# One PSUM bank instead of two for the output products of layer A's segments, and half of the first tail spread moved behind the last rows and their store

## The chip, the core and the metric

The kernel runs on one core of one Trainium2 chip. The metric is the device time of one execution in microseconds (us); the median of the runs counts. A profiled execution gives a trace of its own, with its own time and its span (from its first to its last instruction).

## The reference: what is computed

The input x (2048 rows of 640 values, bf16) goes through four residual layers, A, B, A, B:

```python
x = x + A(layernorm(x)); x = x + B(layernorm(x))
x = x + A(layernorm(x)); x = x + B(layernorm(x))
```

Layer A is attention with a recurrent memory. The rows are cut into 64 segments of 32. For each segment the 8 memory rows and the 32 segment rows are stacked (h, 40 rows), projected to q, k and v with 32 heads of 192 values, masked, put through a softmax, and multiplied by Wo (6144 x 640). The first 8 output rows are the memory of the next segment, the other 32 are the layer's output:

```python
for s in range(n_seg):
    h = jnp.concatenate([mem, xs], axis=1)
    q, k, v = (einsum('btd,dhe->bhte', h, W) for W in (Wq, Wk, Wv))
    p = softmax(where(mask, einsum('bhqe,bhke->bhqk', q, k) * scale, -1e9))
    o = einsum('bhte,hed->btd', einsum('bhqk,bhke->bhqe', p, v), Wo)
    mem = o[:, :M]
    outs.append(o[:, M:])
```

Layer B is linear attention with softmax feature maps over 32 heads of 20 values; it is a chain of large products that needs all rows of layer A's output. The function returns the rows after the fourth layer.

## The kernel before

**The stages.** `run` calls `layer_A` and `layer_B` in turn. `layer_A` consists of `A_pre`, which projects the last 8 rows of every segment in large products, and `A_chain`, which walks through the 64 segments one after the other, because each needs the memory that the one before it leaves. In `A_chain` the order of the instructions on every engine is the order in which they are written (`manual_schedule`); in layer B a scheduler orders them at compile time.

**A segment of the chain.** The 32 heads are worked off in four rounds. A round projects q, k and v (L1092), turns them, forms scores (L1129), exponentials (L1218) and the weighted values (L1142), scales these rows (L1172) and multiplies them by the round's part of Wo into the PSUM tile `ps_w` (L1198, `wo_round`). All four rounds of a segment add into one `ps_w`. The first product into it is issued in round n = 1 of the loop, and the last after the loop. Then the kernel turns `ps_w` (L1371) and adds halves of it (L1373), which gives the memory rows in `hT`. At the start of the next segment `keep_rows(W_done)` reads the same `ps_w` again: two copies on ScalarE into `wh` (L1051) and two additions on VectorE into `orow` (L1054, `under`); `store_rows` sends `orow` to DRAM from the GpSimd queue (L1058). So the tile of one segment is still read when the next has begun, and `ps_w` had two buffers (`bufs=2`).

**The tails.** The output rows 24 to 31 of each segment aren't multiplied in the chain. Their scaled, turned rows (`tail_rows` L1183, `turn_tail` L1187, `store_tail` L1191) go to a DRAM tensor `otb`, and layer B does their products for 16 segments at a time in four blocks tb = 0 to 3 before its own work: `fetch_tails` loads a block (L1388, 1536 KB on the sync queue), `spread_tails` copies it into the layout that TensorE wants (eight copies of 128 x 768 values: two for each round r = 0 to 3, L97 on VectorE for the letter "v", L99 on ScalarE for "s"), and `multiply` runs 48 steps c, each one product of 512 columns into a bank `kv0` or `kv1` (L1421) and one of 128 columns into `ps_post` (L1422). Step c uses the spread of round c // 12. The results leave through `obB` (L1424, L1425, stored by L1427). Later steps of layer B's first part are the block loads of x (L384) and of layer A's output (L389, added on GpSimd by L390), and, in the first layer B only, a fusion of weights (L186, L427, weights loaded by L523) between the steps of blocks 1 and 2.

**The junction.** In the last segment of the chain, block 0 is already fetched during the rounds and its spread is issued with the letters "vvss" straight after the last rows are turned and before the last `wo_round`: rounds 0 and 1 on VectorE, 2 and 3 on ScalarE. After it come the last `wo_round`, four products that only keep TensorE busy (L1205), and after the loop the last tail, `keep_rows` and `store_rows`. The spread of block 1 is issued in layer B behind them. There are two junctions from a layer A to a layer B.

**The banks.** PSUM has eight banks, and the built program shows which tile lies where. In the chain before the change: `ps_qk_q` 0, `ps_qk_k` 1, `ps_w` 2 (even segments) and 3 (odd segments), `ps_v` and `ps_o1` 4, `ps_s` and `ps_idle` 5, `ps_o` 6, `ps_t` 7. In layer B: `kv0` 0, `kv1` 1, `kv2` 2, `ps_post` (and later tiles of the same pool) 3, the other tiles 4 to 7. The last segment has number 63. A tile that lies where an earlier one did waits for the last reader of that one.

Of the kernel before, what the change touches and what calls it, by code (L numbers as in the profile page):

```python
# [8 lines left out]
P = 128  # L9
BF16 = mybir.dt.bfloat16  # L10
F32 = mybir.dt.float32
# [26 lines left out]
def ap3(ap, dims):  # L38
    return bass.AP(tensor=ap.tensor, offset=ap.offset, ap=[list(d) for d in dims])
# [86 lines left out]
class Kernel:  # L126
# [876 lines left out]
    def A_chain(self, xn_dram, at_dram, li, load_slot, piece, late_wo, load_both, wo, low):  # L1003
# [3 lines left out]
        with tc.tile_pool(name=f"A{li}_ch", reuse_waits="tile", bufs=1) as sp, \  # L1007
# [17 lines left out]
            u, w, ut, wt = self.factors()  # L1025
# [10 lines left out]
            def rounds(s):  # L1036
                return range(NR) if s % 2 == 0 else range(NR - 1, -1, -1)
# [9 lines left out]

            def keep_rows(W):
                half = sp.tile([P, 160], F32, name="wh", tag="E")
                for a in range(2):  # L1050
                    nc.scalar.activation(out=half[64 * a:64 * a + 64, :], in_=W[64:P, 160 * a:160 * a + 160], func=ACT.Copy)  # L1051
                for a in range(2):
                    h = slice(64 * a, 64 * a + 64)
                    last = nc.vector.tensor_tensor(out=orow[h, :], in0=W[0:64, 160 * a:160 * a + 160], in1=half[h, :], op=ALU.add)  # L1054
                self.chain_end.append(last)

            def store_rows(s):
                nc.gpsimd.dma_start(out=self.rows_d[32 * s:32 * s + 32, :].rearrange("t (q f) -> q t f", q=4), in_=orow)  # L1058
# [133 lines left out]

            def wo_round(W, r, OT, first, last, part=range(12)):
                for i in part:
                    for g in range(2):
                        q = 32 * (2 * (i % 2) + g)
                        rhs = wo[r, i].rearrange("p (a g f) -> p a g f", a=2, g=2)[:, :, g, :]
                        step = nc.tensor.matmul(W[q:q + 32, 0:320], lhsT=OT[i // 6][:, i % 6 // 2, 32 * (i % 2):32 * (i % 2) + 32],  # L1198
                                         rhs=rhs, start=(first and i < OWN + 2), stop=(last and i in part[-2:]), tile_position=(0, q),
                                         skip_group_check=True)  # L1200
                return step
# [38 lines left out]
            kqs.append(load_kqb(0, rounds(0)[3]))  # L1240
            load_rows(1)
            for s in range(NSEG):
                W = pop.tile([P, 512], F32, name="ps_w", tag="w", bufs=2)
                order = rounds(s)
                L = NR - 1

# [50 lines left out]
                def output_steps(n):  # L1297
                    for j, i in outs[0:n]:
                        wo_round(W, order[j], OTs[j], False, False, range(i, i + 2))
                    del outs[0:n]  # L1300

                for n in range(L):
# [6 lines left out]
                    if n == 1:  # L1309
                        step = wo_round(W, order[0], OTs[0], True, False, range(OWN, 12))  # L1310
                        if s == NSEG - 1:
# [3 lines left out]
                            tails = self.kept_tails  # L1315
# [41 lines left out]
                turn(L, oscs)  # L1357
                output_steps(len(outs))
                if s == NSEG - 1:
                    self.first_tails = tails, [self.spread_tails(0, tails[0], low, "vvss")]  # L1360
                if s + 1 < NSEG:
                    if s + 2 < NSEG:
                        load_rows(s + 2)
# [13 lines left out]
            store_tail(turn_tail(tail_rows(rct, "OTh"), ots[1][:, 0:192]), NSEG - 1, order[L])  # L1377
            keep_rows(W_done)
            store_rows(NSEG - 1)

    def keep_tails(self, tb, low):
        self.kept_tails.append(self.fetch_tails(tb, low))
        return self.tails_load
# [7 lines left out]
    def spread_tails(self, tb, ot, low, engines="vsvs"):  # L1391
        o = 7680 + 12288 * (tb % 2)
        ow = low[:, o + 6144:o + 12288].rearrange("p (r j s x) -> p r j s x", r=4, j=6, x=16)
        for r in range(4):
            for b in range(2):
                at = 192 * (r // 2) + (0 if (r + b) % 2 else 16)
                o = ow[:, r, :, b:16:2, :]
                i = ot[:, b:16:2, at:at + 16]
                i = ap3(i, [list(i.ap[0]), [32, 6], *[list(d) for d in i.ap[1:]]])
                self.ev.copy(out=o, in_=i, eng=engines[r])  # L1400
        return ow
# [64 lines left out]
```

## Time and profile before

| what | value |
|---|---|
| median of 3 runs | 3265.13 us (3263.06, 3265.13, 3274.89) |
| the profiled execution | 3262.61 us, span 3260.9 us |
| mean granted TensorE clock | 0.993 |
| TensorE products busy | 3093.0 us, 95% of the span |
| VectorE, ScalarE, GpSimd busy | 68%, 58%, 43% of the span |
| bytes moved by DMA | 747.58 MB, 229 GB/s on the mean |

In the rows of the profile PE is TensorE's products, PEld its weight loads, DVE VectorE, ACT ScalarE, POOL GpSimd and SPq the sync engine's queue. A row of the timeline has the start in us from the beginning of the span, the duration, the engine, the line, the operation, what is written and read, the shapes and the number of instructions that were merged; in square brackets stands how long the engine sat idle before it and what released it. The four layers take about the stretches 0 to 1374 (A), 1374 to 1643 (B), 1643 to 3003 (A) and 3003 to the end (B).

### The profile page before, as it was taken

The page shows a single profiled execution, that of the slowest core. Times are in us where ns is not written, and L with a number is a line of the kernel's source. Part 1 is how long each engine was busy: PE and PEld are TensorE (multiplying, and loading weights), DVE is VectorE, ACT ScalarE, POOL GpSimd, SP SyncE. Part 2 cuts the span into 40 slices and gives each one's busy share as a digit, 9 for nine tenths or more (in the row PEclk, how much of TensorE's full clock was granted, in tenths as well). Part 3 has the DMA queues.
Part 4 walks back from the last instruction along what each step waited for, and adds up shares of the span by engine and source line. Part 5 has one row for each costly group of instructions (what it writes and reads, how often), then busy time and mean ns, then how long its engine had stood idle before and what let it go on. Part 6 is the DMA issues. An engine that isn't in the chain of part 4 may idle for free.

```text
span 3260.9 us, 140891 instructions
## 1 busy us (share of the span) xinstructions
PE 3093.0 (95%) x59424; PEld 1976.8 (61%) x59730; DVE 2207.3 (68%) x5457; ACT 1882.7 (58%) x4481; POOL 1411.0 (43%) x2920
## 2 busy tenths in 40 slices
PE   9989999999999999899999899999999999998999
PEld 7756666666666666555367566666666666665553
DVE  5557777777777777656643577777777777776565
ACT  3346666666666666546433466666666666666453
POOL 3345555555555554430122355555555555554300
PEclk9999999999999999999999999999999999999999
DMA  8977777777777777840385777777777777778300
GB/s 301 379 274 261 239 252 250 237 256 248 244 260 235 258 248 244 278 155 1 112 318 192 241 239 264 245 256 242 254 253 244 260 238 253 249 245 284 129 1 33
DMA packets 325018, 747.58 MB, mean 229 GB/s; under 512 B 65818, under 2 KB 100274, under 8 KB 321314
## 3 DMA queue, kind: packets, MB, share of 16 engines
q1 hardware_dynamic: 254850, 638.55, 56.3%
q0 software_dynamic: 67616, 86.77, 9.6%
q10 hardware_dynamic: 1920, 13.24, 1.0%
q8 instruction: 469, 7.68, 1.0%
q14 instruction: 163, 1.34, 0.1%
HBM read 668.80 MB, written 77.03 MB: 229 GB/s over the span
## 4 chain that ended last, share of the span: by engine, by line
PE 75%; DMA 11%; DVE 7%; ACT 3%; issue 3%; POOL 0%; SPq 0%; PEld 0%; DVEq 0%; POOLq 0%; ACTq 0%
PE ps_qk_q L1092 12%; PE ps_qk_k L1092 12%; PE ps_v L1092 11%; PE ps_w L1198 10%; PE ps_pre L960 6%; PE ps_s L1129 5%; DMA arena<-in_A_Wv_dram 5%; DMA Vp<-vb 3%; PE ps_pre L989 3%; PE ps_o L1142 3%; PE kv L1421 2%; DMA arena<-wo_rows 2%; DVE raws L1371 2%; PE ps_wo L444 2%; DVE hT L1373 2%
## 5 line engine op out<-in xcount | busy, mean ns | idle before, releaser
L1092 PEld LDWEIGHTS <-hT 128*32 128x32 bf16 x30720 | 790.0, 97 | 422.7 <-issue 40.3
L1112 DVE STREAM_TRANSPOSE QK<-raws 128x512 bf16<-128x512 bf16 (+1 forms) x1152 | 730.4, 642 | 205.5 <-ACT raws L1107 171.4
L1092 PE MATMUL ps_qk_q<-arena,hT 128*32 128x384 bf16 x10240 | 508.5, 327 | 36.3 <-DVE hT L1373 30.4
L1092 PE MATMUL ps_qk_k<-arena,hT 128*32 128x384 bf16 x10240 | 510.0, 328 | 5.4 <-DMA arena<-in_A_Wk_dram 2.3
L1069 POOL COPY QK<-kqb 64x192 bf16<-64x192 bf16 x1024 | 350.4, 342 | 376.7 <-PE ps_s L1129 340.1
L1107 ACT ACTIVATE raws<-ps_qk_k 128x512 bf16<-128x512 f32 (+1 forms) x640 | 313.5, 510 | 253.5 <-PE ps_qk_k L1092 253.5
L1092 PE MATMUL ps_v<-arena,hT 128*32 128x384 bf16 x8192 | 436.0, 327 | 14.3 <-issue 6.8
L1073 POOL DMA_DIRECT2D Vp<-vb x512 | 257.6, 503 | 417.0 <-PE ps_t L1155 252.3
L1172 ACT ACTIVATE raws<-ps_o,rc 128x192 bf16<-128x192 f32 x1024 | 373.7, 420 | 109.8 <-DVE rc L1166 107.5
L1107 ACT ACTIVATE raws<-ps_qk_q 128x512 bf16<-128x512 f32 x512 | 305.7, 597 | 162.5 <-PE ps_qk_q L1092 151.2
L1062 POOL DMA_DIRECT2D kqb<-kqb x512 | 290.6, 568 | 70.9 <-POOL QK L1069 50.2
L1198 PE MATMUL ps_w<-arena,under 128*32 128x320 bf16 x6144 | 306.2, 300 | 11.9 <-issue 8.8
L1121 DVE CAST Vp<-ps_v 64x384 bf16<-64x384 f32 x512 | 286.3, 559 | 38.3 <-ACT Vp L1119 23.0
L1129 PEld LDWEIGHTS <-QK 128*80 128x80 bf16 x4096 | 195.5, 120 | 160.8 <-issue 156.6
L1119 ACT ACTIVATE Vp<-ps_v 64x384 bf16<-64x384 f32 x512 | 246.4, 481 | 55.6 <-PE ps_v L1092 54.8
L1129 PE MATMUL ps_s<-QK 128*80 128x80 bf16 x4096 | 256.4, 210 | 3.8 <-POOL QK L1069 2.8
L1218 ACT ACTIVATE E<-ps_s 80x320 bf16<-80x320 f32 x512 | 217.6, 425 | 30.7 <-PE ps_t L1155 27.7
L1051 ACT ACTIVATE wh<-ps_w 64x160 f32<-64x160 f32 x256 | 76.6, 299 | 266.1 <-DVE raws L1371 256.2
L1058 POOL DMA_DIRECT2D attn<-under x128 | 91.6, 716 | 294.2 <-DVE under L1054 291.3
L960 PEld LDWEIGHTS <-arena 128*128 128x128 bf16 x1920 | 188.4, 98 | 31.6 <-DVE next_xT L97 4.6
L97 DVE CAST arena<-ps_pre 128x512 bf16<-128x512 f32 (+1 forms) x160 | 102.2, 646 | 143.2 <-PE ps_pre L960 96.2
L1142 PE MATMUL ps_o<-Vp,E 80*32 80x193 bf16 x4096 | 179.9, 248 | 18.1 <-DMA Vp<-vb 7.4
(159 smaller groups left out, 4580.7 us busy)
## 6 DMA issues: line engine op xcount, KB each, us to landing
arena<-wo_rows SPq DMA_DIRECT2D x560, 320.0 KB, 5.5
arena<-in_A_Wq_dram SPq DMA_DIRECT2D x427, 384.0 KB, 4.2
arena<-in_A_Wk_dram SPq DMA_DIRECT2D x298, 384.0 KB, 4.7
arena<-in_A_Wv_dram SPq DMA_DIRECT2D x290, 384.0 KB, 6.0
kqb<-kqb POOLq DMA_DIRECT2D x512, 48.0 KB, 4.9
vb<-arena POOLq DMA_DIRECT2D x128, 97.0 KB, 6.1
Vp<-vb POOLq DMA_DIRECT2D x512, 24.2 KB, 4.0
kqb<-arena SPq DMA_DIRECT2D x8, 1536.0 KB, 9.7
```

The costliest lines, as they stand in the source:

```text
L960: nc.tensor.matmul(ps[:, T * i:T * i + T], lhsT=w[b][:, P * c:P * c + P], rhs=xBT[:, b, :], start=(b == 0), stop=(b == KC - 1))
L1062: nc.gpsimd.dma_start(out=kqb[:], in_=self.kqb_d[r, :, s, :])
L1069: nc.gpsimd.tensor_copy(out=o, in_=kqb[h, :].rearrange("p (x c q) -> p x c q", c=3, q=16))
L1073: nc.gpsimd.dma_start(out=Vs[n % 2][64:80, :], in_=self.vb_d[s, r].rearrange("g t f -> (g t) f"))
L1092: last = nc.tensor.matmul(o, lhsT=hT[:, b, :], rhs=rhs, start=(i == 0), stop=(i == KC - 1), tile_position=(0, 32 * g), skip_group_check=True)
L1107: nc.scalar.activation(out=raw[:, c], in_=ps[:, c], func=ACT.Copy)
L1112: nc.vector.transpose(out=o, in_=i)
L1121: nc.vector.tensor_copy(out=o, in_=i)
L1129: nc.tensor.matmul(S[0:80, c0:c0 + 80], lhsT=KT[:, 4 * x + c, :], rhs=QT[:, 4 * x + c, :], start=(c % 2 == 0), stop=(c % 2 == 1), skip_gro ...
L1142: nc.tensor.matmul(O[G][32 * h:32 * h + 32, VH * G:VH * G + 193], lhsT=E[0:80, 80 * h + 32 * G:80 * h + 32 * G + 32], rhs=V[0:80, VH * h:V ...
L1172: nc.scalar.activation(out=out, in_=i, func=ACT.Copy, scale=rc[G])
L1198: step = nc.tensor.matmul(W[q:q + 32, 0:320], lhsT=OT[i // 6][:, i % 6 // 2, 32 * (i % 2):32 * (i % 2) + 32], rhs=rhs, start=(first and i ...
```

## The change

The tile `ps_w` gets the one buffer that its pool has by default, and the spread of block 0 is issued in two halves: rounds 0 and 1 on VectorE where all four stood before, rounds 2 and 3 on ScalarE after the last rows are kept and stored. `spread_tails` leaves out the rounds whose letter is a blank.

```diff
             for s in range(NSEG):
-                W = pop.tile([P, 512], F32, name="ps_w", tag="w", bufs=2)
+                W = pop.tile([P, 512], F32, name="ps_w", tag="w")
...
                 if s == NSEG - 1:
-                    self.first_tails = tails, [self.spread_tails(0, tails[0], low, "vvss")]
+                    self.spread_tails(0, tails[0], low, "vv")
...
             store_tail(turn_tail(tail_rows(rct, "OTh"), ots[1][:, 0:192]), NSEG - 1, order[L])
             keep_rows(W_done)
             store_rows(NSEG - 1)
+            self.first_tails = tails, [self.spread_tails(0, tails[0], low, "  ss")]
...
         for r in range(4):
+            if engines[r:r + 1] in ("", " "):
+                continue
             for b in range(2):
```

In the built program the chain's banks become: `ps_qk_q` 0, `ps_qk_k` 1, `ps_w` 2, `ps_v` and `ps_o1` 3, `ps_s` and `ps_idle` 4, `ps_o` 5, `ps_t` 6; bank 7 is free in the chain. Layer B's banks stay as they were. The order of TensorE's instructions is the same as before. On ScalarE `otr` (L1183) and the two `wh` copies (L1051) of the last segment now stand ahead of the four spread copies. In layer B the scheduler moves a few instructions: VectorE's copies for the spread of block 2 stand behind two more weight copies, a weight store on GpSimd one addition earlier, and in the second layer B the store of block 1's rows (L1427) ahead of one load of layer A's rows (L389) on the sync queue.

## Prediction

> **What bounds the kernel now.** I start at the page: TensorE's products cover 95% of the span, so a change can only pay where TensorE stands still or runs at a lower clock. The change touches two places: the bank of `ps_w` in all 128 segments, and the two junctions from a chain to a layer B. For the chain I ask the instructions of L1054, the last reader of `ps_w`, who waited for them:
>
> ```profile
> span 3260.9 us, 140891 instructions
> PE 3093.0 (95%) x59424; PEld 1976.8 (61%) x59730; DVE 2207.3 (68%) x5457; ACT 1882.7 (58%) x4481; POOL 1411.0 (43%) x2920
> ...
> who waited for it (us, times):
>   POOL attn L1058: 291.3, 126
>   PE ps_post L1422: 15.7, 2
> ```
>
> In 126 segments only the store waited for it, never TensorE. TensorE waited twice, for 15.7 us in all: at the two junctions, with `ps_post`. The timeline of the first junction shows why.
>
> ```profile
> 1372.98 1.03 PE L1205 MATMUL ps_idle<-arena,ident 128*32 128x512 bf16 x4
> ...
> 1376.81 3.04 ACT L99 ACTIVATE arena<-arena 128x768 bf16<-128x768 bf16 x4 [4.81 <-DMA arena<-otb]
> 1376.83 1.16 DVE L97 COPY arena<-arena 128x768 bf16<-128x768 bf16 x4 [4.41 <-DMA arena<-otb]
> 1377.51 0.10 PEld L1421 LDWEIGHTS <-arena 128*128 128x128 bf16 x1 [3.49 <-DVE arena L97]
> 1377.91 0.16 DVE L1178 RECIPROCAL rct<-ps_t 128x1 f32<-128x1 f32 x1
> 1379.76 0.40 ACT L1183 ACTIVATE otr<-ps_t,rct 128x192 bf16<-128x192 f32 x1
> 1380.19 0.61 ACT L1051 ACTIVATE wh<-ps_w 64x160 f32<-64x160 f32 x2
> ...
> 1380.83 0.65 DVE L1054 TENSOR_TENSOR under<-ps_w,wh 64x160 bf16<-64x160 f32 x2 [0.26 <-ACT wh L1051]
> ...
> 1381.62 0.27 PE L1422 MATMUL ps_post<-arena 128*128 128x128 bf16 x1 [7.61 <-DVE under L1054]
> ...
> 1381.68 0.63 PE L1421 MATMUL kv<-arena 128*128 128x512 bf16 x1
> ...
> 1382.11 0.31 PE L1422 MATMUL ps_post<-arena 128*128 128x128 bf16 x1
> ```
>
> TensorE is done with the chain at 1374.01. The tail block lands at 1376.8; VectorE spreads round 0, and TensorE's first weights for block 0 go at 1377.51. The first `kv0` product can follow; `ps_post` can't. It lies in bank 3, the last segment's `ps_w` too, so it waits until `keep_rows` has read that. `keep_rows` is late because its ScalarE copies stand behind four spread copies (3.04 us) and the tail row. The idle time thus has two halves: up to 1377.5 it is the load, from there to 1381.62 the bank. The second junction is the same:
>
> ```profile
> 3002.05 1.03 PE L1205 MATMUL ps_idle<-arena,ident 128*32 128x512 bf16 x4
> ...
> 3007.10 0.10 PEld L1421 LDWEIGHTS <-arena 128*128 128x128 bf16 x1 [4.01 <-DVE arena L97]
> 3007.50 0.16 DVE L1178 RECIPROCAL rct<-ps_t 128x1 f32<-128x1 f32 x1
> ...
> 3011.20 0.26 PE L1422 MATMUL ps_post<-arena 128*128 128x128 bf16 x1 [8.12 <-DVE under L1054]
> ```
>
> Three more stretches of the timeline are needed for the parts: the last reader of `ps_o1` at the junction, a segment in the middle of the chain, and the pace of TensorE in block 0 at full clock.
>
> ```profile
> 1371.59 0.41 ACT L1172 ACTIVATE raws<-ps_o,rc 128x192 bf16<-128x192 f32 x1
> ```
>
> ```profile
> 1000.64 0.65 DVE L1054 TENSOR_TENSOR under<-ps_w,wh 64x160 bf16<-64x160 f32 x2
> ...
> 1007.45 0.73 PE L1198 MATMUL ps_w<-arena,under 128*32 128x320 bf16 x16
> ```
>
> ```profile
> 1384.80 0.38 PE L1421 MATMUL kv<-arena 128*128 128x512 bf16 x1
> ...
> 1385.07 0.38 PE L1421 MATMUL kv<-arena 128*128 128x512 bf16 x1
> ```
>
> **Part 1, one bank.** At the junction `ps_post` now lies where the chain had `ps_v` and `ps_o1`. The last reader of that bank on ScalarE is L1172 of the last round, which ends at 1372.0, before TensorE is idle at all. So the first `ps_post` follows its `kv0` product. The weight load at 1377.51 takes 0.10, and from a `kv0` product to its `ps_post` pass 0.43 us at half clock (1381.68 to 1382.11) and about half of that, 0.21, at full clock. Junction one, where the clock is still full: 1377.51 + 0.10 + 0.21 = 1377.82 against 1381.62, **3.80 us earlier**. Junction two, at half clock by then: 3007.10 + 0.10 + 0.43 = 3007.63 against 3011.20, **3.57 us earlier**. Sum 7.4.
>
> In the chain the single bank adds a dependence: the first product of a segment must follow the last read of the segment before. In the segment at 1000 us the read ends at 1001.29 and the first product starts at 1007.45, so 6.16 us are to spare. TensorE issues in order, and that product waits already for its round's transposes on VectorE, behind L1054 in the same queue, so the built program gets no further wait there. I cost it at nothing. Without that cover each 0.1 us would cost 12.6 us over 126 segments.
>
> **Part 2, the spread in halves.** VectorE is unchanged: rounds 0 and 1 end at 1377.99, `rct` at 1378.07. ScalarE is then free, so the tail row runs from 1378.1 to 1378.5, `wh` to 1379.13, L1054 to about 1379.8, and the two stores leave 1.65 us earlier. Nobody on TensorE waits for these now. The four copies follow on ScalarE from 1379.13, two by 1380.7 and all by 1382.2, instead of 1379.85. TensorE needs rounds 2 and 3 at steps 24 and 36. At the fastest pace of the trace (a `kv0` product each 0.27 us, 1384.80 to 1385.07) step 24 comes at 1377.6 + 24 x 0.27 = 1384.1: 3.4 us of cover for round 2 and 5.1 for round 3. Cost nothing.
>
> So part 1 alone should give the whole gain, part 2 alone 1.65 us a junction (`keep_rows` ends earlier, the bank wait stays), and both together no more than part 1.
>
> **What is queued behind.** The rows that bear on it: the loads of blocks 2 and 3, block 1's spread, the ends of blocks 0 and 1, the first later idle time of TensorE; then the time to landing of a block, and that of the fusion weights (L523), their issue and their first use.
>
> ```profile
> 1382.89 4.35 SPq L1388 DMA_DIRECT2D arena<-otb  x2
> ...
> 1383.84 3.04 ACT L99 ACTIVATE arena<-arena 128x768 bf16<-128x768 bf16 x4 [3.04 <-issue]
> ...
> 1396.08 0.69 DVE L1424 CAST obB<-kv 128x512 bf16<-128x512 f32 x1 [11.12 <-PE kv L1421]
> ...
> 1414.45 0.69 DVE L1424 CAST obB<-kv 128x512 bf16<-128x512 f32 x1 [1.65 <-PE kv L1421]
> ...
> 1450.81 1.52 PE L444 MATMUL ps_v<-arena 128*128 128x500 bf16 x10 [1.01 <-ACT arena L457]
> ```
>
> ```profile
> arena<-otb SPq DMA_DIRECT2D x4, 1536.0 KB, 10.9
> ```
>
> ```profile
> DMA to landing us min/median/max: 16.4/16.4/16.4
> ```
>
> ```profile
> 1371.33 3.51 SPq L523 DMA_DIRECT2D arena<-in_B_wqkv_dram  x2
> ...
> 1396.73 0.44 PE ps_t L186 x6
> ```
>
> Block 2's load waits on the sync queue for ScalarE's spread of block 0. The queue reaches it at 1382.89 and the spread ends at 1382.2: 0.7 us to spare, and were it gone, the load has time until block 2's products.
>
> Is the earlier start given back? Block 1's spread ends at 1386.9 (ScalarE), and block 1 starts after block 0, at 1396.1 now and 1392.3 then: 5.4 us to spare. The fusion weights land 16.4 us after their issue, 1387.7 to 1391.2 for the two loads, against a first use at 1396.73 now and near 1392.9 then. Block 2's load lands near 1382.89 + 10.9 = 1393.8; its spread would like to begin about then, but its products begin only near 1410.6. From there TensorE runs on to 1449.8 without a wait on a load, so the shift stays. The moved instructions (two VectorE copies, a weight store on GpSimd before one of its additions, a row store ahead of a row load on the sync queue) concern rows that are used only after block 2. Nothing.
>
> **The clock.** Windows across the junctions show the granted clock in the third column from the right:
>
> ```profile
> 1377.80:1378.20 0.40, 0.00 (x0) 0.00 (x0) 0.27 (x2) 0.40 (x1) 0.00 (x0) 0.58 1.07 417
> ...
> 1384.40:1384.80 0.40, 0.40 (x5) 0.16 (x3) 0.40 (x3) 0.40 (x2) 0.00 (x0) 0.64 1.06 358
> ...
> 3005.80:3006.20 0.40, 0.00 (x0) 0.00 (x0) 0.00 (x0) 0.00 (x0) 0.00 (x0) 0.78 1.01 372
> ...
> 3016.20:3016.60 0.40, 0.40 (x4) 0.17 (x3) 0.00 (x0) 0.36 (x1) 0.00 (x0) 0.92 0.95 298
> ```
>
> A mean of 0.58 between 1 and 0.5 puts the fall at 1377.86 and, by the same reckoning, the rise at 1384.69; at the second junction 3006.02 and 3016.26. The distances, 6.83 and 10.24 us, are two and three steps of 3.41: the clock seems to be set on a grid of that step. Before, TensorE works 3.07 and 5.06 us at half clock, which loses 1.53 + 2.53 = 4.06 us. After, if the clock falls again and TensorE's start meets the grid at random, one step of 3.41 on the mean: 1.71 a junction, 3.42 together, a gain of 0.6. Bounds: no fall at either (+4.1), or 5.1 us slow at both (-1.1).
>
> [...]
>
> **The sum.** 7.4 + 0.6 = 8.0 us, 0.25%. The profiled execution took 3262.61 (the span and 1.7 around it), which gives 3254.6. The median shown, 3265.13, lies 2.5 above it, which gives 3257.1. I take the middle, **3256.0**.
>
> **The rivals.** One row of a table of windows is wanted for the second; its last but one column is the DMA engines' share.
>
> ```profile
> 1396.00:1400.00 4.00, 3.84 (x36) 2.50 (x35) 2.71 (x8) 2.54 (x5) 0.00 (x0) 1.00 0.97 328
> ```
>
> 1. The clock stays up. After the change TensorE is idle from 1374.01 to 1377.5 and from 3003.08 to 3007.1, 3.5 and 4.0 us, hardly more than a step. [...] Gain 7.4 + 4.06 = 11.5: 3251.1 from the profiled time, 3253.6 from the median. Against it: both falls in the trace come 3.9 and 2.9 us after TensorE stops. [...] 0.15 for both junctions; one alone lies in the forecast.
> 2. Given back later: loads that nobody waits for now end last, since the DMA engines are full until about 1400 (a share of 0.97 in the window below). Gain 0 to 4: 3259 to 3265. For it: the only 1.7 us between the later weights and the fusion. Against it: they land in order of issue, the first 5 us early. 0.09.
> 3. It doesn't do what it says: TensorE stalls at another reader and gains nothing: 3262.6 to 3265.1. Against it stands the ScalarE row at 1371.59. 0.04.
> 4. Slower: the single bank binds in the chain. It decides where the last read of `ps_w` comes 6.16 us later than now: each 0.064 us beyond costs 126 x 0.064 = 8 us and eats the gain, and 0.2 us a segment would give 3257 + 25 = 3282. Against it: L1054 directly follows L1051 in every segment, and VectorE does it before the first turn of a round. 0.04.
>
> **How the numbers follow.** Forecast 0.68, rivals 0.15, 0.09, 0.04, 0.04. What a measurement of this kernel can tell from no change is about 0.5%, 16 us. The forecast and rivals 1 to 3 lie within it; only rival 4 and a median high in the spread of the runs give slower, 0.03, and nothing that I can work out gives 16 us faster, 0.02. Same 0.95. The range: rival 1 from the profiled time, 3251, less one for the spread of runs, to no gain from the median, 3265, plus one: 3250 to 3266.
>
> **What would show it.** Right: `ps_post` at the junctions starts 0.2 to 0.5 us after the first weight load and waits for the spread (L97), not for L1054; `wh` (L1051) starts near 2 us after the tail block landed, ahead of ScalarE's spread; no wait of TensorE on ScalarE at steps 24 and 36; a segment of the chain is as long as before. Wrong: a TensorE wait on L1051 or L1054 in the chain, or new idle time at the fusion or before block 2.

## The result, and the profile after

| what | before | after |
|---|---|---|
| median of 20 runs each, on one chip | 3268.23 us (3259.6 to 3276.76) | 3259.12 us (3249.09 to 3268.4) |
| ratio, 95% interval | | 0.9967 (0.9956 to 0.9978) |
| the profiled execution | 3262.61 us, span 3260.9 | 3255.46 us, span 3253.7 |
| mean granted clock | 0.993 | 0.994 |

The change makes the kernel faster by 0.33%, 10.8 us (7.2 to 14.4). The interval leaves out 1, but the size lies under the 0.5% that the prediction took as its bound, so by that bound it is "the same". The forecast was 3256.0 and a gain of 8.0.

The first row of the page, and who waited for the readers and writers of `ps_w` (us, times), of the kernel after:

```profile
span 3253.7 us, 140890 instructions
```

```profile
who waited for it (us, times):
  POOL attn L1058: 289.7, 126
  ACT wh L1051: 254.9, 122
  DVE raws L1371: 133.4, 126
  DVE under L1054: 1.9, 6
```

No row of TensorE is left: the two waits of 15.7 us in all are gone, and in the chain none has come in their place. What TensorE still waits at the junctions, 8.0 us in all, is for VectorE's spread. Who waited for L97 in the kernel after:

```profile
who waited for it (us, times):
...
  PE ps_post L1425: 8.0, 2
```

Line numbers in layer B are now 3 higher: L1424 is the `kv0` product and its weights, L1425 `ps_post`, L1427 `obB`. The timeline of the first junction (start, duration, engine, line; idle time and releaser in brackets):

```profile
1372.27 1.03 PE L1205 MATMUL ps_idle<-arena,ident 128*32 128x512 bf16 x4
...
1376.20 1.17 DVE L97 COPY arena<-arena 128x768 bf16<-128x768 bf16 x4 [4.50 <-DMA arena<-wo_rows]
1376.88 0.10 PEld L1424 LDWEIGHTS <-arena 128*128 128x128 bf16 x1 [3.58 <-DVE arena L97]
...
1377.29 0.31 PE L1425 MATMUL ps_post<-arena 128*128 128x128 bf16 x1 [3.99 <-DVE arena L97]
...
1377.92 0.61 ACT L1051 ACTIVATE wh<-ps_w 64x160 f32<-64x160 f32 x2
...
1378.56 3.04 ACT L99 ACTIVATE arena<-arena 128x768 bf16<-128x768 bf16 x4
1378.57 0.65 DVE L1054 TENSOR_TENSOR under<-ps_w,wh 64x160 bf16<-64x160 f32 x2 [0.26 <-ACT wh L1051]
...
1391.66 0.69 DVE L1427 CAST obB<-kv 128x512 bf16<-128x512 f32 x1 [6.76 <-PE kv L1424]
```

`ps_post` starts 0.41 us after the first weight load instead of 4.11, and what releases it is the spread (L97), not L1054, which runs 1.3 us later. ScalarE does the two `wh` copies first and the four spread copies (L99) behind them. The second junction:

```profile
2999.82 1.02 PE L1205 MATMUL ps_idle<-arena,ident 128*32 128x512 bf16 x4
...
3004.62 0.10 PEld L1424 LDWEIGHTS <-arena 128*128 128x128 bf16 x1 [3.77 <-DVE arena L97]
...
3004.85 0.28 PE L1425 MATMUL ps_post<-arena 128*128 128x128 bf16 x1 [4.01 <-DVE arena L97]
...
3019.49 0.69 DVE L1427 CAST obB<-kv 128x512 bf16<-128x512 f32 x1 [7.28 <-PE kv L1424]
```

I cut a junction in three: the gap (end of the fourth idle product to the first weight load), the lag (from there to `ps_post`) and the block (`ps_post` to VectorE's `obB` copy). This table is worked out from the timelines of all profiled kernels but e5 and e6; each junction is gap / lag / block = sum.

| kernel | first junction | second junction | both |
|---|---|---|---|
| before | 3.50 / 4.11 / 14.46 = 22.07 | 4.02 / 4.10 / 15.43 = 23.55 | 45.62 |
| after | 3.58 / 0.41 / 14.37 = 18.36 | 3.78 / 0.23 / 14.64 = 18.65 | 37.01 |
| after, again (h1) | 3.84 / 0.23 / 14.65 = 18.72 | 3.08 / 0.23 / 14.65 = 17.96 | 36.68 |
| e1: one bank alone | 2.24 / 0.24 / 12.96 = 15.44 | 4.02 / 0.40 / 15.34 = 19.76 | 35.20 |
| e2: spread in halves alone | 3.28 / 2.48 / 15.49 = 21.25 | 3.47 / 2.48 / 15.54 = 21.49 | 42.74 |
| e3: two banks, `ps_post` elsewhere | 3.40 / 0 / 14.52 = 17.92 | 3.78 / 0 / 14.46 = 18.24 | 36.16 |
| e4: after, TensorE kept busy | 2.97 / 0.23 / 12.97 = 16.17 | 3.71 / 0.24 / 12.96 = 16.91 | 33.08 |
| h2: the same kernel as e4 | 3.33 / 0.23 / 12.97 = 16.53 | 2.97 / 0.23 / 12.97 = 16.17 | 32.70 |
| e7: block 0 loaded in halves | 1.48 / 0.23 / 12.97 = 14.68 | 3.12 / 0.23 / 14.64 = 17.99 | 32.67 |
| e8: e7, TensorE kept busy | 1.30 / 0.23 / 12.97 = 14.50 | 1.54 / 0.23 / 12.97 = 14.74 | 29.24 |
| h3: the same kernel as e8 | 1.95 / 0.23 / 12.97 = 15.15 | 1.47 / 0.23 / 12.97 = 14.67 | 29.82 |

The two junctions give 45.62 - 37.01 = 8.61 us, 7.57 of it in the lag. The spans differ by 7.2. Count a chain from its first L1092 product (L1093 in e7, e8 and h3) to its first idle product: the first chain is 0.73 shorter (1202.21 to 1201.48), the second 2.36 longer (1193.38 to 1195.74), the rest 0.2 shorter. That a chain moves by this much means little: over the profiles of e1 to e4, e7, e8 and h1 to h3, whose chains hold nearly the same instructions, the first chain takes 1198.6 to 1207.9 us and the second 1193.8 to 1205.0. The clock does not make this spread: summed over windows of 6 us, TensorE is at half speed for 10.2 us in the first chain of h2, the shortest (1198.6), and for 10.1 us in that of e2 (1207.8). What does is open. A gain of 8 is as large as that spread, which is why only many runs side by side show it in the time.

### The profile page after: what moved, and what is told of

Same layout as the page of the kernel before. It is cut to its first block, busy times and chain, and to the rows that moved or that the text cites. A ratio compares the mean times of both kernels' runs of the same rounds, so it can differ in the third digit from the quotient of the medians.

```text
span 3253.7 us, 140890 instructions
## 1 busy us (share of the span) xinstructions
PE 3095.3 (95%) x59424; PEld 1980.2 (61%) x59730; DVE 2208.8 (68%) x5457; ACT 1883.0 (58%) x4481; POOL 1410.7 (43%) x2920
## 4 chain that ended last, share of the span: by engine, by line
PE 75%; DMA 11%; DVE 8%; issue 3%; ACT 3%; POOL 0%; SPq 0%; PEld 0%; DVEq 0%; POOLq 0%; ACTq 0%
PE ps_qk_q L1092 12%; PE ps_qk_k L1092 12%; PE ps_v L1092 11%; PE ps_w L1198 10%; DMA arena<-in_A_Wv_dram 6%; PE ps_pre L960 6%; PE ps_s L1129 5%; PE ps_o L1142 3%; PE ps_pre L989 3%; PE kv L1424 2%; DVE raws L1371 2%; PE ps_wo L444 2%; DMA Vp<-vb 2%; DMA arena<-wo_rows 2%; DVE hT L1373 2%
## 5 line engine op out<-in xcount | busy, mean ns | idle before, releaser
L1092 PEld LDWEIGHTS <-hT 128*32 128x32 bf16 x30720 | 792.6, 97 | 422.7 <-issue 43.0
L1092 PE MATMUL ps_qk_q<-arena,hT 128*32 128x384 bf16 x10240 | 510.4, 327 | 38.2 <-DVE hT L1373 31.1
L1092 PE MATMUL ps_qk_k<-arena,hT 128*32 128x384 bf16 x10240 | 511.7, 328 | 3.1 <-issue 1.2
L1092 PE MATMUL ps_v<-arena,hT 128*32 128x384 bf16 x8192 | 435.2, 326 | 15.2 <-DMA arena<-in_A_Wv_dram 7.2
L1051 ACT ACTIVATE wh<-ps_w 64x160 f32<-64x160 f32 x256 | 76.6, 299 | 264.8 <-DVE raws L1371 254.9
L97 DVE CAST arena<-ps_pre 128x512 bf16<-128x512 f32 (+1 forms) x160 | 102.2, 646 | 143.5 <-PE ps_pre L960 96.4
```

What stands on the lines that cost most here:

```text
L1092: last = nc.tensor.matmul(o, lhsT=hT[:, b, :], rhs=rhs, start=(i == 0), stop=(i == KC - 1), tile_position=(0, 32 * g), skip_group_check=True)
```

## The experiments

The theory: TensorE waited at the junctions on the bank that `ps_post` shared with the last segment's `ps_w`, and nothing else of the change matters. The rivals: the order of the spread pays; the granted clock pays; the single bank costs in the chain and eats a part; what was won is given back behind block 0. Each kernel computes the whole output. Where a run is given as a number near 1, it is its time over that of the kernel before, run beside it, with the 95% interval.

### e1 and e2: each part alone

e1 is the kernel before with the first line of the diff; e2 is the changed kernel without it:

```diff
-                W = pop.tile([P, 512], F32, name="ps_w", tag="w", bufs=2)
+                W = pop.tile([P, 512], F32, name="ps_w", tag="w")
```

> The single bank alone; the spread of block 0 stays whole, with the letters vvss, before the last products. Theory (the bank is what TensorE waited for): ps_post starts 0.2 to 0.5 us after the first weight load at both junctions although keep_rows still ends 3 to 4 us after that load; from the end of the four idle products to VectorE's first obB copy about 18.5 us at both junctions, as in the changed kernel (18.4 and 18.7) and not 22.1 and 23.5 as before; about 8 us less than before in time. Rival (the order on ScalarE is what counts): ps_post keeps waiting for L1054, 22 to 23.5 us, no gain.

> The spread in halves alone; ps_w keeps its two banks. Theory: keep_rows ends 1.6 to 1.8 us earlier after the load has landed, and ps_post still waits for L1054, so each junction gets 1.7 us shorter, up to 0.8 more or less by the clock's grid: 20.4 and 21.8 us from the idle products to the first obB copy, 3 to 4 us in time. Rival (the order on ScalarE is what counts): 18.5 us at both, 8 us.

Measured: e1 0.9974 (0.9956 to 0.9991), e2 0.9992 (0.9976 to 1.0008). The first junction of e1 (old line numbers), then of e2:

```profile
1374.47 0.10 PEld L1421 LDWEIGHTS <-arena 128*128 128x128 bf16 x1 [2.24 <-DVE arena L97]
1374.71 0.22 PE L1422 MATMUL ps_post<-arena 128*128 128x128 bf16 x1 [2.48 <-DVE arena L97]
```

```profile
1381.19 0.10 PEld L1424 LDWEIGHTS <-arena 128*128 128x128 bf16 x1 [3.28 <-DVE arena L97]
1382.88 0.65 DVE L1054 TENSOR_TENSOR under<-ps_w,wh 64x160 bf16<-64x160 f32 x2 [0.26 <-ACT wh L1051]
1383.67 0.27 PE L1425 MATMUL ps_post<-arena 128*128 128x128 bf16 x1 [5.77 <-DVE under L1054]
```

With one bank the lag is 0.24 and 0.40 us with the old order of the spread, and 0.41 and 0.23 with the new one. With two banks `ps_post` still waits for L1054; the new order only lets L1054 end earlier: the lag falls from 4.11 to 2.48, 1.63 us a junction against 1.65 predicted. So the bank carries the lag's whole gain, and the spread adds nothing to it. In the time e1 can't be told from the whole change, nor e2 from no change.

### e3: the bank wait removed in another way

Two banks for `ps_w` as before, but in layer B the pool of `ps_post` is opened ahead of the pool of `kv`, so `ps_post` lies in bank 0:

```diff
-        with tc.tile_pool(name=f"B{li}_kv", ...) as kvp, \
-                tc.tile_pool(name=f"B{li}_pt", ...) as ptp, \
+        with tc.tile_pool(name=f"B{li}_pt", ...) as ptp, \
+                tc.tile_pool(name=f"B{li}_kv", ...) as kvp, \
```

> The kernel before with both banks of ps_w and the old spread; only layer B's pool with ps_post is opened ahead of the one with kv0 to kv2, so that ps_post lies in bank 0, kv0 in 1, kv1 in 2 and kv2 in 3. Theory (it is a matter of which tile meets the last segment's ps_w): same gain as the single bank alone, about 18.5 us a junction and 8 us in time, because bank 3 then belongs to kv2, which is first written some 50 us later. Rival (one bank in the chain makes the chain itself shorter, or the gain is spread of runs): junctions as before, 22 to 23.5 us, no gain.

Measured: 0.9979 (0.9967 to 0.9991), junctions 36.16. The first one:

```profile
1382.22 3.51 PE L1422 MATMUL ps_post<-arena 128*128 128x128 bf16 x36 [3.41 <-DVE arena L97]
1385.51 4.47 PEld L1421 LDWEIGHTS <-arena 128*128 128x128 bf16 x22
1385.54 0.65 DVE L1054 TENSOR_TENSOR under<-ps_w,wh 64x160 bf16<-64x160 f32 x2 [0.26 <-ACT wh L1051]
```

The scheduler now puts 36 `ps_post` products first, and none of them waits for `keep_rows`. The `kv` products follow with no wait on it in the profile. The sum of the junctions is that of the changed kernel within 0.9 us. So it isn't the number of buffers that pays: it is that the new tile no longer lies on one with late readers. Nor does one bank cost anything in the chain that shows: e3 with two is no faster than e1 with one (0.9979 against 0.9974).

### e4 and h2: TensorE kept busy until the load has landed

```diff
-                for _ in range(4):
+                for _ in range(4 if s + 1 < NSEG else 18):
                     keep_busy(idle, 512)
```

> The changed kernel with 18 idle products in the last segment instead of 4; 14 more take about 3.0 us and fill most of the 3.6 to 3.8 us in which TensorE waits for the tail block. Theory (what is left at the junction is the load, and the clock that fell meanwhile): the granted clock stays at 1.0 across both junctions, the first block runs at full pace, 1.5 to 1.7 us less at each junction than in the changed kernel, about 3 us in time. Rival 1 (the load bounds everything, and the clock costs nothing because block 1 waits for its own spread anyway): no change in when block 2 starts. Rival 2: the idle products end after the block has landed and delay it: 0 to 0.5 us more a junction.

> The run with 18 idle products once more, on the same chip. Theory (the chains vary by themselves, and the clock's price at the junctions stays saved): junctions 33 us in sum, 12 us less than before, 3 to 4 less than the changed kernel. Rival (a junction without a fall of the clock makes the chain after it slower; both profiles without a fall at either junction had the longest second chains, 1205.7 and 1206.0 us against 1194 to 1202): second chain again near 1206, time as the changed kernel.

Measured: e4 0.9968 (0.9952 to 0.9984), h2 0.9973 (0.9958 to 0.9987). The second junction of e4, and two windows across it (the clock third from the right):

```profile
3014.53 4.05 PE L1205 MATMUL ps_idle<-arena,ident 128*32 128x512 bf16 x18
...
3019.27 0.10 PEld L1424 LDWEIGHTS <-arena 128*128 128x128 bf16 x1 [0.69 <-DVE arena L97]
```

```profile
3018.60:3019.30 0.70, 0.00 (x0) 0.03 (x2) 0.70 (x3) 0.00 (x0) 0.00 (x0) 1.00 1.07 409
3019.30:3024.00 4.70, 4.50 (x34) 2.69 (x36) 1.55 (x6) 4.07 (x7) 1.33 (x2) 1.00 1.03 416
```

The clock is 1.00 in both windows, and block 0 takes 12.96 or 12.97 us in all four junctions of these two runs. That is the price of the fallen clock: 14.37 - 12.97 = 1.40 and 14.64 - 12.97 = 1.67 us in the changed kernel. The 3.1 us don't show in the time; the interval of either run is wider than that. A fall came at another place too: at the first junction of e4 the clock was at 0.50 under the chain's last products, before the idle ones began at 1375.88:

```profile
1372.50:1375.50 3.00, 3.00 (x54) 1.89 (x49) 1.02 (x4) 0.73 (x2) 0.00 (x0) 0.50 0.96 355
```

### e5 and e6: using up the cover in the chain

`keep_rows` and `store_rows` move from the start of the segment to just ahead of the exponentials of round 1, where the next product into `ps_w` is due. e5 does it in the changed kernel, e6 in e2's kernel with two banks:

```diff
-                    keep_rows(W_done)
...
-                    store_rows(s - 1)
...
+                    if n == 1 and s > 0:
+                        keep_rows(W_done)
+                        store_rows(s - 1)
```

> The changed kernel (one bank) with keep_rows moved later in every segment: from the segment's start to just before the exponentials of round n = 1, where the segment's first output products follow at once. This uses up the 6.16 us between the last read and the next first product. Theory (the single bank is free only by that distance): TensorE now waits for L1054 in each of 126 segments, by the row of a segment at 1008.97 us some 1.5 to 2 us (ScalarE's copy of the rows 0.60, the two wh copies 0.61, the two additions 0.65 come before the product instead of long ago); a segment takes 1.5 to 2 us more and the kernel 190 to 250 us more than the changed one. Rival (the bank costs nothing wherever its readers stand): the same time as the two-bank run beside it.

> The same late keep_rows with two banks for ps_w and the spread in halves. Theory: no wait of TensorE on L1054; the exponentials come later because wh shares their buffer, which may cost 0.2 to 0.8 us a segment, 25 to 100 us in all; the difference to the one-bank run, 100 to 200 us, is the price of the bank. Rival (moving keep_rows costs by itself, the bank nothing): both runs equally slow.

Measured: e5 3402.29 us, 1.0420 (1.0396 to 1.0443); e6 3346.18, 1.0249 (1.0223 to 1.0275). Who waited for L1054 in e5, and for the exponentials `E` in e6, in the changed kernel and in e5:

```profile
  PE ps_w L1198: 204.9, 126
```

```profile
  PEld L1142: 217.0, 252
```

```profile
  PEld L1142: 36.3, 113
```

```profile
  PEld L1142: 32.2, 126
```

The wait of rival 4 exists: made late, the reads of the one bank hold TensorE 126 times for 204.9 / 126 = 1.63 us. But its size was misjudged. e5 lies about 146 us above the changed kernel (0.0453 x 3263.66 = 148 by the ratios, 3402.29 - 3256.13 = 146 by the medians, which are of two chips), and only 3402.29 - 3346.18 = 56 us above e6. In e6 TensorE doesn't wait for the bank, yet the move delays ScalarE's exponentials, and the weight loads of the weighted values wait for them 217 us. In e5 they wait for them only 32.2 us, no more than in the changed kernel, which fits that TensorE stands at the bank at that time: the two waits lie largely side by side. So the 204.9 us in the table of waits weren't 204.9 us of time. The 56 are a rough price, for e6 keeps the bank wait at the junctions (by the ratios of e2 and of the changed kernel, 0.9992 and 0.9967, about 8 us).

### e7, e8 and h3: a shorter gap

What was left of the idle time is the load, so here block 0 comes as two loads, one for rounds 0 and 1 and one for rounds 2 and 3 (so `release` lets one load more go); e8 and h3 also issue 9 idle products instead of 4:

```diff
-        self.otb_d = dram.tile([P, NSEG, 384], BF16, name=f"otb{li}")
+        self.otb_d = dram.tile([2, P, NSEG, 192], BF16, name=f"otb{li}")
...
-                held.append(lambda: self.keep_tails(0, low))
+                held.append(lambda: self.keep_tails(0, low, (0,)))
+                held.append(lambda: self.keep_tails(0, low, (1,)))
...
-                            self.release(step, 12)
+                            self.release(step, 13)
```

> The changed kernel with block 0 of the tails loaded in two halves: the tails are kept in DRAM as two planes (rounds 0 and 1, rounds 2 and 3), and the first plane (768 KB) is issued ahead of the second. Theory (what is left at the junction is the landing of that load): at about 370 GB/s half of the bytes land some 2 us earlier, TensorE's first weight load comes 1.5 to 2 us after the idle products instead of 3.6 to 3.8, the first obB copy 16 to 17 us after them instead of 18.4 and 18.7, or 15 if the clock then doesn't fall; about 4 us less in time than the changed kernel, 6 if the clock stays. ScalarE's spread waits for the second plane and still ends before step 24. Rival (the DMA engines are full and share their time between the queued loads, so both planes land when the whole did): no change.

> Both planes as in the run with the load in halves, and 9 idle products instead of 4 in the last segment (1.1 us more). Theory: clock at 1.0 across both junctions, first block at full pace (13.2 us from the first weight load to the first obB copy), the first obB copy 14.8 to 15.3 us after the fourth idle product; 6 to 7 us less than the changed kernel, 14 to 16 us less than before, about 0.45%. Rival (load not earlier): as the run with 18 idle products at best, or slower clocks as in the changed kernel.

Measured: e7 0.9968 (0.9951 to 0.9984), e8 0.9968 (0.9953 to 0.9983). The gap did get shorter, to 1.48 and 3.12 us in e7 (1.5 to 2 were expected) and to 1.30 and 1.54 in e8, but the 4 to 7 us of time expected beyond the changed kernel don't show. Then the changed kernel, the kernel of e4 and the kernel of e8 once more, on one chip:

> The changed kernel once more, beside the two that follow on one chip. Theory: junctions (fourth idle product to first obB copy) 37 us in sum, some 8.5 us less than before in time. If the chains' own spread (their length differed by up to 12 us between the profiles so far) hides it: anything from 3 to 14.

> The run with the load in halves and 9 idle products once more, on the same chip. Theory: junctions 29 us in sum, 16 us less than before, 7 to 8 less than the changed kernel. Rival (a junction without a fall makes the second chain slower): second chain again near 1206, 10 us less than before at most.

Measured: h1 3256.13 us, 0.9966 (0.9951 to 0.9980); h2 3257.03; h3 3255.87, 0.9963 (0.9946 to 0.9980). The first junction of h3:

```profile
1374.36 2.10 PE L1206 MATMUL ps_idle<-arena,ident 128*32 128x512 bf16 x9
...
1377.34 0.10 PEld L1432 LDWEIGHTS <-arena 128*128 128x128 bf16 x1 [0.87 <-DVE arena L97]
```

The junctions of h3 are 36.68 - 29.82 = 6.9 us shorter than those of h1, but the time isn't: the means are 3255.1 and 3256.2, 1.1 less with a standard error of 2.3. A part is lost behind block 0: from the first `obB` of layer B to the next chain h3 takes 414.11 us against 412.77, and behind the second junction 235.67 against 234.24, 2.8 in all. Only 0.3 of it shows in block 1 (from its `obB` to that of block 0, 18.69 against 18.37; in e8 19.42). The rest, 2.5, is no more than two falls of the clock cost that h1 does not have: from 1596 to 1656 us TensorE is 13.6 us at half speed in h3 and 10.2 in h1, one step of 3.41 more, and behind the second junction there is a fall near 3191 us, of one step again. Each step costs half of it, about 1.7 us (block 0 of the changed kernel paid 1.40 and 1.67 for one). The fall in the second stretch of h3, then the same place in h1:

```profile
3186.00:3196.00 10.00, 9.32 (x29) 3.12 (x29) 4.18 (x8) 4.61 (x8) 0.00 (x0) 0.83 0.00 0
```

```profile
3197.00:3207.00 10.00, 9.32 (x35) 3.38 (x34) 5.77 (x10) 6.01 (x10) 0.00 (x0) 1.00 0.00 0
```

4.1 us remain against 1.1 with its error of 2.3, and the runs don't settle whether that is chance. I had also feared that a second chain runs slower where the clock never fell: h2's took 1202.92 against 1199.66, but h3's 1195.18, so that falls. No version measured here is shown to be faster than the changed kernel.

## Why the prediction was right, point by point

**Part 1** said 3.80 and 3.57 us; the lag fell by 3.70 and 3.87, 7.57 against 7.4. At the first junction the clock had fallen just before (1376.72, against 1376.88 for the weights), so the first `ps_post` came 0.41 and not 0.31 after the weights; at the second it hadn't yet (3004.87, against 3004.85 for `ps_post`). e1 and e3 show that the bank is the cause. That the chain loses nothing was right too: no wait of TensorE on a reader of `ps_w`. In a segment near 1000 us the read ends at 1002.81 and the next product starts at 1008.97:

```profile
1002.16 0.65 DVE L1054 TENSOR_TENSOR under<-ps_w,wh 64x160 bf16<-64x160 f32 x2
...
1008.97 0.73 PE L1198 MATMUL ps_w<-arena,under 128*32 128x320 bf16 x16
```

That is again 6.16 us to spare. The price that the prediction put on the lack of that cover, 12.6 us for each 0.1 us, was too high: e5's 1.63 us a segment would cost 205 by it, and cost some 56.

**Part 2** said that both parts give no more than part 1, and part 2 alone 1.65 a junction. Shown by e2 (1.63 and 1.62), and TensorE waited for no spread copy of ScalarE. `wh` starts 1.72 us after the first spread copy (1376.20 to 1377.92), where about 2 was forecast.

**Given back**, rival 2: from the first `obB` of a block to that of the next the changed kernel takes 18.36 us at the first junction against 18.37 before, and 51.6 against 51.8 from the first block's to the fourth's. To the next chain it is 412.42 against 412.59, and behind the second junction 234.21 against 234.27. The whole shift passes on, so rival 2 falls for this change; with a further 7 us, block 1 gives back 1.05 us in e8 and 0.3 in h3.

**The clock** said one step of 3.41 us at half speed at each junction, instead of two and three, a gain of 0.6. Four windows of the changed kernel, two at each junction:

```profile
1376.40:1376.80 0.40, 0.00 (x0) 0.00 (x0) 0.40 (x3) 0.00 (x0) 0.00 (x0) 0.90 1.04 391
1379.80:1380.20 0.40, 0.40 (x3) 0.24 (x2) 0.00 (x0) 0.40 (x2) 0.40 (x1) 0.59 1.09 461
3004.80:3005.20 0.40, 0.35 (x2) 0.22 (x2) 0.38 (x3) 0.00 (x0) 0.00 (x0) 0.59 1.07 421
3008.00:3009.00 1.00, 1.00 (x8) 0.60 (x7) 0.00 (x0) 1.00 (x2) 0.00 (x0) 0.86 0.95 378
```

By the same reckoning as in the prediction it falls at 1376.72 and rises at 1380.13, falls at 3004.87 and rises at 3008.28: one step of 3.41 each time. The block became 0.09 and 0.79 us shorter, 0.88 against 0.6. One step at each junction was forecast as a mean, and that both hit it is partly luck: in e1, with the same single bank, block 0 took 12.96 us (no fall) at one junction and 15.34 (two steps, 3005.54 to 3012.37) at the other. Rival 1 falls: that gaps of 3.5 and 4.0 us might leave the clock up was a supposition, and at all four junctions of the two profiles of the changed kernel, with gaps of 3.08 to 3.84 us, the block takes 14.37 to 14.65 us, not 12.97.

**The sum** was 8.0, of the profiled time. The junctions gave 8.61, 0.16 of it from the gap, which the load sets. The profiled times differ by 7.15, and the runs by 10.8 (7.2 to 14.4): the chains' own spread lies between these. The median came out 3.1 above the 3256.0, and so had the median before, which is 3265.13 of three runs and 3268.23 of twenty: that distance is one of the base. That the gain in time lies so near 8.0 is partly luck; the 8.61 at the junctions is the firmer agreement.

## What to carry to other kernels

When a stage begins, look at which old tiles its first PSUM tiles lie on, and who reads those last: a late read of a few hundred ns cost 4.1 us here, since it stood behind other work in its engine's queue, and one buffer fewer or another order of the pools removed it. In a table of waits, ask what would end next if a wait were gone: e5's 204.9 us were worth 56. When two profiles differ by less than the spread of their longest stage, compare them stage by stage, and leave the time to many runs side by side.

## What the runs showed of the hardware that was not expected

The granted clock fell after idle gaps as short as 3.08 us, less than one step of 3.41 (the second junction of h1, where block 0 then took 14.65 us and not 12.97; 3.12 in e7, block 14.64):

```profile
3007.67 1.03 PE L1205 MATMUL ps_idle<-arena,ident 128*32 128x512 bf16 x4
...
3011.78 0.10 PEld L1424 LDWEIGHTS <-arena 128*128 128x128 bf16 x1 [3.08 <-DVE arena L97]
```

In e7 the fall even came when block 0 was under way. Its second junction has the last idle product's end at 3000.63 and the first weight load at 3003.75, and the 0.72 in this window puts the fall at 3004.58:

```profile
3004.40:3004.80 0.40, 0.40 (x5) 0.20 (x3) 0.00 (x1) 0.38 (x2) 0.00 (x0) 0.72 0.97 371
```

So TensorE had worked for 0.83 us again when the clock fell. In the kernels with 4 idle products, every gap from 3.08 to 4.02 us was followed by a slow block of 14.37 to 15.54 us (in the kernel before and in e2 TensorE then stood longer still, for the bank); after gaps of 1.48 and 2.24 the block took its 12.97 or 12.96.

The clock also falls late in the first layer B, where TensorE is busy, and not the same in each run. Windows of 10 us of the changed kernel, then of h2:

```profile
1606.00:1616.00 10.00, 9.52 (x38) 3.33 (x36) 7.05 (x19) 3.85 (x10) 1.55 (x3) 0.86 0.14 50
1616.00:1626.00 10.00, 9.32 (x55) 4.00 (x54) 7.19 (x28) 5.12 (x10) 4.87 (x10) 1.00 0.34 119
```

```profile
1606.00:1616.00 10.00, 8.83 (x32) 3.18 (x32) 7.62 (x23) 7.43 (x17) 1.62 (x3) 0.81 0.14 49
1616.00:1626.00 10.00, 9.89 (x49) 3.85 (x47) 6.55 (x20) 2.15 (x4) 5.14 (x10) 0.85 0.38 127
```

Summed over the six windows from 1596 to 1656 us (twice the missing clock times 10 us), TensorE is 10.2 us at half speed in the profiles before and after, and 23.8 in h2, about three and seven steps of 3.41. h2's stretch from the first layer B's `obB` to the next chain is 7.1 us longer than that of the changed kernel (419.57 against 412.42), about half of the 13.6 us between them. That fits a part of the spread of the runs; why the clock falls there was not tried.
